# Attention and two expert layers on one core: another order of the opening's loads, more buffers for the first block, weights of the first pair in halves, a decode without its clamp

## The chip, the cores and the metric

The kernel runs on one core of one Trainium2 chip. The metric is the device time of one execution in microseconds (us). A core has TensorE (PE, matrix products; its weight loads are shown as PEld), VectorE (DVE), ScalarE (ACT), GpSimd (POOL) and SyncE (SP), which here only issues transfers. Each engine works through its own list of instructions in the order in which they were written, and waits on semaphores. Transfers run on 16 DMA engines.

## The reference

Three parts follow each other. Attention over 4 batches, 8 heads, 576 positions and 64 columns for a head adds a coarse part (means over 4 positions, full attention over 144 of them, each result used 4 times) and a local part (positions less than 4 apart):

```python
out_d = sm_attn(q_d, k_d, v_d)          # q_d ...: means over 4 positions
out_up = np.repeat(out_d, factor, axis=2)
mask = np.abs(pos[:, None] - pos[None, :]) < factor
...
return (out_up + out_local).astype(np.float32)
```

Its output is 2304 tokens of 512 columns. The first layer computes `g = h * tanh(softplus(h))` with `h = x @ w_in` (512 to 2048 columns) and `g @ w_out`. The second computes `h * softmax(h)` with 1024 columns, a layer norm with gain and a last product. The weights arrive as 64-bit floats, the rest as 32-bit.

## The kernel before, in words

The 2304 tokens are 18 units of 128 tokens; `BLOCKS = [4, 3, 3, 4, 4]` gathers them into five blocks. For each block the attention (`local`, per unit; `coarse`, per batch and pair of heads p) writes x into a tile as a high and a low part. Then 16 slots follow, one for each 128 columns of the 2048 (f = 0 to 15): `chunk_in` multiplies (L630, 12 matmuls: 4 pieces of the contraction, 3 products of high and low parts) and runs the activation on ACT and DVE, and `chunk_out` multiplies back (L658, 12 matmuls). `SEGS` runs block 0 with f = 0 to 9 first (slots 0 to 9), then all of block 1 (slots 10 to 25), then the rest of block 0 and the other blocks. The second layer (`tile_in`, `tile_out`) comes last.

**Weights.** Two values of f share a tile, a pair j. `first_weights` loads the 64-bit words of a pair (1 MB for `wi`, 1 MB for `wo`), `decode` makes 32-bit floats of them with an activation and four DVE passes (L540 is the clamp, L544 a shift, L546 and L548 bring in other bits), and `split` (L552, L553) makes the high and the low part. Pairs 0 to 4 are needed in slots 0 to 9, pairs 5, 6 and 7 from slots 20, 22 and 24. A load waits for the decode two tiles before it (`pace`).

**One local unit.** Loads of k, q (L321, L322) and four small ones of v (L326); 64 small matmuls for the scores (L352); mask, maximum, exponentials (L373) and norm on DVE and ACT; four transposes (L391); 64 small matmuls for the values (L409); the sum with the coarse part (L419); high part (L430) and low part (L432) of x. The first block's units ("early") share two score tiles and write their values to two PSUM banks with the tag "at". The values of a unit need all four coarse parts of its batch.

**One coarse part of batch 0.** Loads of q and k (L450) and, for two p at once, of v (L452); sums over 4 positions on DVE (L453 to L460); scores (L483, 12 matmuls), maximum, exponentials (L490), norm (L498), six transposes (L512), values (L525, 8 matmuls), copy (L529). For block 1 and later the sums over 4 positions are done by transfers that accumulate, issued by POOL (L263).

**The order of the work.** `Plan` keeps every operation with its engine, an estimated cost, a due time in slots ("want") and its buffers. `Plan.run` plays the program once with these costs: each engine always takes the ready operation with the lowest due time whose buffers are free. The resulting order is what is written, engine by engine. So the constants `CLOAD0`, `LOAD0`, `COARSE0`, `LOCAL0` and their spacings (opening), `NEXT` (attention of the next block) and `WANT` (weight pairs) set the order and nothing else; due times of the opening are negative. Transfers of SP go to one queue in order of issue.

## Time and profile before

| | us |
|---|---|
| median of 3 runs | 742.5 (737.35 to 745.17) |
| profiled execution, whole | 748.06 |
| its span, first to last instruction | 745.9 |
| PE busy | 700.8 |
| DVE busy | 475.3 |
| ACT busy | 485.7 |

The span is that of the profiled execution and is what views of the trace are measured in. Busy time of PE is modelled for pipelined matmuls and is no measure of how full the array is. "<-issue" behind an idle time says that the engine waited for nothing that the profile shows.

### The profile page before, as it was taken

How to read it: one execution, taken by the hardware profiler on the slowest of the kernel's cores; microseconds unless marked ns; L12 is line 12 of the kernel's file. 1: busy time of each engine (PE TensorE's matmuls, PEld its weight loads, DVE VectorE, ACT ScalarE, POOL GpSimd, SP SyncE). 2: the span in 40 equal slices, each digit the busy share in tenths (PEclk: the TensorE clock that was granted, in tenths of full speed). 3: DMA queues.
4: the chain of work that ended last, by engine and by line, in shares of the span. 5: the costliest groups of instructions: out<-in, count | busy, mean ns of one | idle time of the engine just before them, and what ended most of it. 6: DMA issues, size and time to landing. Idle time of an engine off the chain costs nothing.

```text
span 745.9 us, 14393 instructions
## 1 busy us (share of the span) xinstructions
PE 700.8 (94%) x5584; PEld 589.1 (79%) x5584; DVE 475.3 (64%) x1038; ACT 485.7 (65%) x1143; POOL 71.6 (10%) x86
## 2 busy tenths in 40 slices
PE   3656998999989999999999999999999999999997
PEld 2445676889988899999788888888888788888886
DVE  6767997597745536765656655655556776666662
ACT  2764977677767667786766856776754555555542
POOL 2031343012420002120000000000000000000000
PEclk9656999999989999999999999999999999999999
DMA  8887676466633127761524223310415534443331
GB/s 245 260 232 209 145 169 159 157 155 152 126 61 107 55 46 178 182 156 58 177 80 134 69 93 125 121 50 11 145 59 168 161 130 162 141 155 129 128 139 43
DMA packets 75532, 98.35 MB, mean 132 GB/s; under 512 B 6536, under 2 KB 58120, under 8 KB 75464
## 3 DMA queue, kind: packets, MB, share of 16 engines
q1 hardware_dynamic: 63432, 83.61, 35.4%
q0 software_dynamic: 9440, 9.10, 8.7%
q10 hardware_dynamic: 2592, 4.72, 1.6%
q8 instruction: 44, 0.72, 0.4%
q14 instruction: 24, 0.20, 0.1%
HBM read 73.81 MB, written 23.59 MB: 131 GB/s over the span
## 4 chain that ended last, share of the span: by engine, by line
PE 85%; DVE 4%; ACT 4%; DMA 4%; issue 2%; SPq 1%; ACTq 0%
PE h L630 26%; PE y L658 25%; PE at L808 12%; PE y L699 12%; PE at L409 3%; DMA ku<-in_ku_dram 2%; PE at L699 1%; DMA g<-in_qu_dram 1%; PE at L352 1%; PE at L483 1%; SPq L265 1%; PE at L525 1%; PE at L512 1%; DMA vu<-in_vu_dram 1%; PE at L391 1%
## 5 line engine op out<-in xcount | busy, mean ns | idle before, releaser
L630 PE MATMUL h<-x,wi 128*128 128x512 f32 (+1 forms) x960 | 217.7, 377 | 6.5 <-DVE e L644 6.5
L658 PE MATMUL y<-g,wo 128*128 128x512 f32 (+1 forms) x960 | 218.2, 375 | 0.0
L630 PEld LDWEIGHTS h<-x,wi 128*128 128x128 f32 x960 | 176.3, 191 | 33.3 <-DVE e L644 8.6
L658 PEld LDWEIGHTS y<-g,wo 128*128 128x128 f32 x960 | 174.5, 190 | 24.4 <-issue 1.6
L808 PE MATMUL at<-wi,wo 128*128 128x512 f32 x432 | 100.6, 389 | 0.0
L808 PEld LDWEIGHTS at<-wi,wo 128*128 128x128 f32 x432 | 81.0, 188 | 16.8
L699 PE MATMUL y<-wi,raw 128*128 128x512 f32 x384 | 89.9, 390 | 1.1 <-DVE raw L691 1.1
L638 ACT ACTIVATE e<-h 128x512 f32<-128x512 f32 (+1 forms) x80 | 44.2, 552 | 66.0 <-PE h L630 65.4
L699 PEld LDWEIGHTS y<-wi,raw 128*128 128x128 f32 x384 | 71.9, 188 | 16.7 <-DVE raw L691 1.5
L644 DVE SCALAR_TENSOR_TENSOR e<-e,h 128x512 f32<-128x512 f32 (+1 forms) x80 | 50.3, 630 | 32.0 <-ACT e L643 31.3
L647 DVE TENSOR_TENSOR g<-e,g 128x512 fp32r<-128x512 f32 (+1 forms) x80 | 50.6, 634 | 23.9 <-ACT g L646 23.4
L639 DVE TENSOR_SCALAR e<-e 128x512 f32<-128x512 f32 (+1 forms) x80 | 31.8, 398 | 53.3 <-ACT e L638 53.2
L640 ACT ACTIVATE e<-e,ones 128x512 f32<-128x512 f32 (+1 forms) x80 | 54.3, 680 | 17.3 <-DVE e L639 16.9
L646 ACT CAST g<-e 128x512 fp32r<-128x512 f32 (+1 forms) x80 | 45.9, 575 | 28.2 <-DVE e L644 27.9
L642 ACT ACTIVATE e<-e,ones 128x512 f32<-128x512 f32 (+1 forms) x80 | 54.2, 679 | 1.7
L263 POOL DMA_DIRECT2D qkd<-in_qkc_dram x36 | 35.6, 992 | 141.1 <-DMA qkd<-in_qkc_dram 84.3
L643 ACT ACTIVATE e<-e 128x512 f32<-128x512 f32 (+1 forms) x80 | 46.9, 586 | 1.1
L263 POOL DMA_DIRECT2D vd<-in_vc_dram x36 | 36.3, 1028 | 58.0 <-DMA vd<-in_vc_dram 48.0
L373 ACT ACTIVATE sm<-sm,nm 128x40 f32<-128x40 f32 x120 | 37.6, 315 | 4.6 <-DVE nm L367 4.6
L813 ACT COPY ys<-at 128x512 f32<-128x512 f32 x18 | 10.6, 589 | 41.3 <-PE at L808 41.3
L725 ACT ACTIVATE wo<-y,nm 128x1024 f32<-128x1024 f32 x16 | 17.9, 1118 | 22.3 <-DVE nm L723 22.3
L540 DVE TENSOR_SCALAR ys<-ys 128x512 f32<-128x512 f32 (+1 forms) x36 | 18.6, 517 | 17.4 <-ACT ys L539 17.3
(155 smaller groups left out, 822.2 us busy)
## 6 DMA issues: line engine op xcount, KB each, us to landing
raw<-in_w_dram SPq DMA_DIRECT2D x24, 512.0 KB
zscr<-wo SPq DMA_DIRECT2D x17, 512.0 KB
wo<-zscr SPq DMA_DIRECT2D x68, 128.0 KB
wi<-in_w_dram SPq DMA_DIRECT2D x6, 1024.0 KB
wo<-in_w_dram SPq DMA_DIRECT2D x6, 1024.0 KB
qkd<-in_qkc_dram POOLq DMA_DIRECT2D x36, 144.0 KB, 4.3
ku<-in_ku_dram SPq DMA_DIRECT2D x15, 320.0 KB
vu<-in_vu_dram SPq DMA_DIRECT2D x60, 80.0 KB
```

What stands on the lines that cost most here:

```text
L263: return op("pool", nbytes / DMA_RATE, want, lambda: nc.gpsimd.dma_start(out_(), in_(), accum_op=ALU.add), r, w, after=after)
L630: mm(h()[:, :N], w()[:, f % 2, a, 128 * c:128 * c + 128], x()[:, b, c, :N], start=(n == 0), stop=(n == 11))
L638: act(act_us(N), s + 0.1, lambda: nc.scalar.activation(e(), h()[:, :N], AF.Exp), [h], [eb])
L640: act(act_us(N, 0.09), s + 0.1, lambda: nc.scalar.activation(e(), e(), AF.Square, bias=ones()[:, 0:1]), [ones], [eb])
L642: lambda: nc.scalar.activation(e(), e(), AF.Ln, scale=0.5, bias=ones()[:, 1:2]), [ones], [eb])
L643: act(act_us(N), s + 0.1, lambda: nc.scalar.activation(e(), e(), AF.Exp, scale=-1.0), [], [eb])
L644: dve(dve_us(N), s + 0.2, lambda: nc.vector.scalar_tensor_tensor(e(), e(), 1.0, h()[:, :N], op0=ALU.subtract, op1=ALU.mult), [h], [eb])
L646: act(act_us(N), s + 0.2, lambda: nc.scalar.copy(g()[:, 0, :N], e()), [eb], [g])
L647: dve(dve_us(N), s + 0.2, lambda: nc.vector.tensor_tensor(g()[:, 1, :N], e(), g()[:, 0, :N].bitcast(F32), op=ALU.subtract), [eb], [g])
L658: mm(y[d2]()[:, d, :N], w()[:, f % 2, a, c:c + 128], g()[:, b, :N], start=(f == fs[0] and n == 0), stop=(f == fs[-1] and n == 2))
L699: mm(part(m), x()[:, a, c, :], w()[:, i, b, :], start=(n == 0), stop=(n == 11))
L808: mm(o(), ln()[:, a, k, :], w()[:, i, b, :], start=(n == 0), stop=(n == 23))
```

## The change

The seven coarse loads of batch 0 are issued as one group ahead of the units' loads, with due times of their own; the weights of pair 0 come after the units, each in two halves with decode and split of their own, so that a slot needs only the half that it reads. The four early units have a score tile each (one of its own and three parts of one tile), pairs of small columns each, and the odd ones write their values into a "y" PSUM tile instead of two "at" banks. The norm of the early coarse parts goes from DVE (L498) to ACT, as three activations with a scale for each partition. `decode` drops the clamp: the activation multiplies by 2^-112 instead of taking the absolute value, and the two bit masks are adapted. All constants of the order are new. In `Plan`, small transfers of POOL (the masks) no longer take the place of others in the played program, and a tile is held as long as one of its parts is.

The diff, cut to its core:

```diff
-LEAD = 2.5
-EARLY = -84
-CLOAD0 = -90
-LOAD0 = -86
-EI = 2.5
-COARSE0 = -80
-CSPC = 5.0
-CDT = 2
-LOCAL0 = -76
-LSPC = 4.0
-CLOAD = 4.0
+LEAD = 2.2
+EARLY = -95.5
+CLOAD0 = -108.6
+VLOAD = [-115.1, -87.3]
+LOAD0 = -77.4
+FIRST = {'wi': (-67.7, -66.3), 'wo': (-64.9, -40.0)}
+EI = 9.9
+COARSE0 = -111.0
+CSPC = 1.1
+CDT = 7.9
+LOCAL0 = -105.5
+LSPC = 1.4
+CLOAD = 12.8
...
-NEXT = {0: (0.0, 6.0, -3.0, 0.8), 26: (-3.0, 4.0, -14.0, 2.0), 32: (2.0, 10.0, 4.0, 1.2), 48: (2.0, 10.0, 4.0, 1.2)}
-WANT = [0, 2, 4, 6, 8, 13, 16, 20]
+NEXT = {0: (0.6, 7.5, -8.4, 0.2), 26: (-4.7, 4.4, -13.4, 0.2), 32: (-3.9, 7.5, -5.0, 1.7), 48: (1.4, 10.4, 2.8, 3.4)}
+WANT = [6.9, 4.6, 4.5, 5.8, -4.5, 13.8, 34.8, 28.7]
...
+SHIFT = 2.0 ** -112
...
+        bufs.update({id(b.of): b.of for b in list(bufs.values()) if isinstance(b, View)})
...
+                        if eng == "pool" and cost < 0.1:
+                            heapq.heappush(done, (at[eng] + 3.0, pick, False))
+                            continue
...
-    sms = [S([UQ, 2, 2, 2, 64], *t) for t in (("sm0", 1), ("wi", 8))]
+    sms = [S([UQ, 2, 2, 2, 64], "sm0", 1)]
+    smw = S([UQ, 3, 2, 2, 2, 64], "wi", 8)
+    sms += [View(smw, lambda t, i=i: t[:, i]) for i in range(3)]
+    small = S([UQ, 96], "nm", 2)
...
-        tl = LOAD0 + LSPC * u if early else t0 - 2.5
+        tl = LOAD0 + 3.0 * u if early else t0 - 2.5
...
-        sm = sms[u % 2 if soon else 0]
+        sm = sms[u if early else u % 2 if soon else 0]
...
-        nm = S([UQ, 96], "nm", 2)
-        su = S([UQ, 16], "su", 2)
+        if early:
+            nm, su = (View(small, lambda t, c=c: t[:, c:c + 8]) for c in (16 * u, 16 * u + 8))
+        else:
+            nm = S([UQ, 96], "nm", 2)
+            su = S([UQ, 16], "su", 2)
...
-        o = [P("at"), P("at")]
+        if early and u % 2:
+            oy = P("y")
+            o = [View(oy, lambda t, par=par: t[:, par]) for par in range(2)]
+            of = [oy]
+        else:
+            o = of = [P("at"), P("at")]
...
-            dma(CLOAD0 + p, qk4, lambda: qkc[0, :, :, p].rearrange("r d s t -> d r s t"), w=[qk4], nbytes=589824)
-            if p % 2 == 0:
-                dma(CLOAD0 + p + 0.5, v8, lambda: vc[0, :, :, p:p + 2].rearrange("r k p g d -> k r p g d"), w=[v8], nbytes=589824)
...
-        dve(dve_us(432), t0 + 0.4 * dt, norm_b, [su], [smb])
+        def norm_c():
+            for c in range(3):
+                nc.scalar.activation(sm()[:, c, :], sm()[:, c, :], AF.Copy, scale=su()[:, c:c + 1])
+
+        if early:
+            act(0.7, t0 + 0.4 * dt, norm_c, [su], [smb])
+        else:
+            dve(dve_us(432), t0 + 0.4 * dt, norm_b, [su], [smb])
...
-        act(act_us(n), want, lambda: nc.scalar.activation(xf(), high().bitcast(F32), AF.Abs), [raw], [x])
+        act(act_us(n), want, lambda: nc.scalar.activation(xf(), high().bitcast(F32), AF.Copy, scale=SHIFT), [raw, *hold], [x])
         dve(dve_us(n, True), want, lambda: nc.vector.tensor_scalar(
-            xf(), xf(), HIGH_MIN, HIGH_MAX, op0=ALU.max, op1=ALU.min), [], [x])
-
-
-        dve(dve_us(n, True), want, lambda: nc.vector.tensor_scalar(
-            xi(), xi(), 3, 0x3FFFFFF8, op0=ALU.logical_shift_left, op1=ALU.bitwise_and), [], [x])
+            xi(), xi(), 3, 0x7FFFFFF8, op0=ALU.logical_shift_left, op1=ALU.bitwise_and), [*hold], [x])
...
+    def opening_weights(tag, src, want):
+
+        w = S([128, 2, 2, 512], tag, 8, F32R)
+        x = S([128, 2, 512], "ys", 2)
+        raw = S([128, 2, 512, 2], tag, 8, I32)
+        for i in range(2):
+            ri, xi, wv = (View(b, lambda t, i=i: t[:, i]) for b in (raw, x, w))
+            dma(FIRST[tag][i], ri, lambda i=i: words(src[:, i], "k (n two) -> k n two"),
+                r=[raw, w], w=[ri], nbytes=524288)
+            last = decode(xi, lambda t: t, ri, 512, want + i, [x, raw])
+            act(act_us(512), want + i + 0.1, lambda xi=xi, wv=wv: nc.scalar.copy(wv()[:, 0], xi()), [xi, x, w], [wv])
+            dve(dve_us(512), want + i + 0.1, lambda xi=xi, wv=wv: nc.vector.tensor_tensor(
+                wv()[:, 1], xi(), wv()[:, 0].bitcast(F32), op=ALU.subtract), [xi, x, w], [wv])
+            ready_w[tag, i] = [wv]
+        pace.append(last)
+        return w
...
+        qk4s.append(S([128, 4, 2, 144], *(("x1", 1), ("x0", 1), ("wo", 8), ("wo", 8))[p]))
+        dma(CLOAD0 + 0.1 * p, qk4s[p], lambda p=p: qkc[0, :, :, p].rearrange("r d s t -> d r s t"), w=[qk4s[p]], nbytes=589824)
+    for i in range(2):
+        v8s.append(S([72, 4, 2, 2, 128], "wo", 8))
+        dma(VLOAD[i], v8s[i], lambda i=i: vc[0, :, :, 2 * i:2 * i + 2].rearrange("r k p g d -> k r p g d"), w=[v8s[i]], nbytes=589824)
```

## Rows read from the trace of the kernel before

**Rows 1.** Page: busy time of the engines; shares of the chain that ended last.
```profile
PE 700.8 (94%) x5584; PEld 589.1 (79%) x5584; DVE 475.3 (64%) x1038; ACT 485.7 (65%) x1143; POOL 71.6 (10%) x86
...
PE 85%; DVE 4%; ACT 4%; DMA 4%; issue 2%; SPq 1%; ACTq 0%
```

**Rows 2.** Busy time by stretches: stretch, length, engines, TensorE clock, DMA share, GB/s.
```profile
0.00:30.00 30.00, 15.92 (x231) 10.86 (x232) 20.53 (x47) 11.02 (x38) 4.57 (x12) 0.93 0.94 265
30.00:65.30 35.30, 18.03 (x533) 14.53 (x530) 25.60 (x53) 22.71 (x95) 10.82 (x12) 0.50 0.85 226
65.30:139.30 74.00, 69.70 (x589) 54.56 (x588) 56.30 (x101) 55.89 (x134) 21.73 (x24) 0.94 0.60 146
139.30:225.40 86.10, 82.66 (x557) 77.40 (x557) 62.67 (x125) 64.24 (x152) 21.45 (x24) 0.96 0.57 138
225.40:745.90 520.50, 514.53 (x3683) 431.75 (x3681) 310.25 (x716) 331.84 (x727) 13.03 (x14) 1.00 0.37 115
```

**Rows 3.** TensorE's timeline, opening: start, us, operation, count, idle before it and releaser.
```profile
27.19 0.93 PE L352 MATMUL y<-g 64*32 64x40 f32 x64 [0.86 <-DMA g<-in_qu_dram]
...
37.72 0.85 PE L409 MATMUL at<-wo,vu 40*64 40x32 f32 x19 [0.28 <-issue]
39.92 1.11 PE L391 MATMUL h<-ident,wi 128*128 128x128 f32 x4 [1.34 <-DVE wi L383]
40.96 0.94 PE L352 MATMUL y<-wi 64*32 64x40 f32 x64
41.83 1.28 PE L409 MATMUL at<-wo,g 40*64 40x32 f32 x39
46.62 0.87 PE L409 MATMUL at<-wo,g 40*64 40x32 f32 x25 [3.51 <-issue]
...
64.62 0.71 PE L352 MATMUL at<-ku,qu 64*32 64x40 f32 x36 [3.32 <-issue]
65.26 7.98 PE L630 MATMUL h<-x,wi 128*128 128x512 f32 x24
```

**Rows 4.** DMA view, instruction queue: whole span; then 34:36, 43:45, 62:65, 65:67.
```profile
q8 instruction: 44, 0.72, 0.4%
...
q8 instruction: 1, 0.02, 3.2%
...
q8 instruction: 1, 0.02, 2.9%
...
q8 instruction: 1, 0.02, 2.0%
...
q8 instruction: 1, 0.02, 3.0%
```

**Rows 5.** SP's timeline: issue of the fourth unit's values.
```profile
33.12 3.46 SPq L265 DMA_DIRECT2D wi<-in_vu_dram  x4
```

**Rows 6.** DVE's timeline: the first pass over loaded data.
```profile
5.39 0.76 DVE L453 TENSOR_TENSOR x<-x 128x576 f32<-128x576 f32 x1 [3.41 <-DMA x<-in_qkc_dram]
```

**Rows 7.** Groups by line and shape: busy us, mean ns of one; idle before, releaser.
```profile
L540 DVE TENSOR_SCALAR ys<-ys 128x1024 f32<-128x1024 f32 x12 | 8.4, 700 | 3.7 <-ACT ys L539 3.7
L546 DVE SCALAR_TENSOR_TENSOR ys<-wi,ys 128x1024 int32<-128x1024 int32 x6 | 7.4, 1235 | 0.1
L553 DVE TENSOR_TENSOR wi<-ys,wi 128x1024 fp32r<-128x1024 f32 x16 | 19.5, 1221 | 9.3 <-ACT wi L552 9.3
L498 DVE TENSOR_TENSOR wo<-wo,csu 128x432 f32<-128x432 f32 x8 | 4.8, 603 | 0.1
L490 ACT ACTIVATE wo<-y,cnm 128x144 f32<-128x144 f32 x12 | 4.4, 377 | 11.8 <-DVE cnm L503 11.8
```

**Rows 8.** TensorE's timeline later on: two waits for DVE.
```profile
76.67 3.02 PE L630 MATMUL h<-x,wi 128*128 128x512 f32 x12 [1.81 <-DVE e L644]
...
208.51 2.98 PE L630 MATMUL h<-x,wi 128*128 128x384 f32 x12 [1.95 <-DVE e L644]
```

More of the change, by code (lines that the diff above doesn't have):

```diff
@@ L1 @@
 import heapq
-import struct
 from contextlib import ExitStack
@@ L410, in values @@
                                at()[r, 2 * h2 + a, GQ * g:GQ * g + GQ], start=True, stop=True)
-        passed["x", u] = pe(1.2 if early else 0.7, t0 + 0.7 * dt, values, [v, at] + ups, o + [xf], after=gate_x)
+        passed["x", u] = pe(1.9 if early else 0.7, t0 + 0.7 * dt, values, [v, at] + ups, of + [xf], after=gate_x)
         for par in range(2):
@@ L423, in add @@
                         op=ALU.add)
-            dve(dve_us(256) + 0.04, t0 + 0.8 * dt, add, [o[par]] + ups, [xf])
+            dve(dve_us(256) + 0.04, t0 + 0.8 * dt, add, [of[par % len(of)]] + ups, [xf])
         x = xt[i]
@@ L434 @@
     v8s = []
+    qk4s = []
     def coarse(b, p, t0, dt):
@@ L442, in coarse @@
         if early:
-            qk4 = S([128, 4, 2, 144], *(("x1", 1), ("x0", 1), ("wo", 8), ("wo", 8))[p])
-            if p % 2 == 0:
-                v8s.append(S([72, 4, 2, 2, 128], "wo", 8))
+            qk4 = qk4s[p]
             v8 = v8s[p // 2]
@@ L529, in coarse, with decode @@
         act(0.17, t0 + 0.8 * dt, lambda: nc.scalar.copy(up[b]()[:, p, :], o()[:, :144]), [o], [up[b]])
-    def decode(x, part, raw, n, want):
+    def decode(x, part, raw, n, want, hold=()):
         low = lambda: raw()[..., 0]
@@ L537, in decode @@
         xi = lambda: part(x()).bitcast(I32)
[L539 removed]
+        act(act_us(n), want, lambda: nc.scalar.activation(xf(), high().bitcast(F32), AF.Copy, scale=SHIFT), [raw, *hold], [x])
         dve(dve_us(n, True), want, lambda: nc.vector.tensor_scalar(
[L541 to L545 removed]
+            xi(), xi(), 3, 0x7FFFFFF8, op0=ALU.logical_shift_left, op1=ALU.bitwise_and), [*hold], [x])
         dve(dve_us(n), want, lambda: nc.vector.scalar_tensor_tensor(
[L547 removed]
+            xi(), low(), 29, xi(), op0=ALU.logical_shift_right, op1=ALU.bitwise_or), [raw, *hold], [x])
         return dve(dve_us(n), want, lambda: nc.vector.scalar_tensor_tensor(
[L549 removed]
+            xi(), high(), -0x80000000, xi(), op0=ALU.bitwise_and, op1=ALU.bitwise_or), [raw, *hold], [x])
     def split(w, x, want):
@@ L560 @@
     pace = []
+    ready_w = {}
+    def opening_weights(tag, src, want):
[13 more added lines that the diff above has]
+        return w
     def first_weights(j, tag, src, want, after):
@@ L632, in g1 @@
                     n += 1
-        g1_op[s] = pe(12 * (N + 32) / 2400, s, g1, [w, x], [h], after=[g1_op.get(s - 1)])
+        g1_op[s] = pe(12 * (N + 32) / 2400, s, g1, [w, x, *ready_w.get(("wi", f), [])], [h], after=[g1_op.get(s - 1)])
         eb = S([128, NMAX], "e", 3)
@@ L659, in g2 @@
                            start=(f == fs[0] and n == 0), stop=(f == fs[-1] and n == 2))
-            pe(6 * (N + 32) / 2400, s + 1.7, g2, [w, g], [y[d2]])
+            pe(6 * (N + 32) / 2400, s + 1.7, g2, [w, g, *ready_w.get(("wo", f), [])], [y[d2]])
     def block_end(i, s, N, y, more):
@@ L829 @@
     for p in range(4):
+        qk4s.append(S([128, 4, 2, 144], *(("x1", 1), ("x0", 1), ("wo", 8), ("wo", 8))[p]))
[3 more added lines that the diff above has]
+        dma(VLOAD[i], v8s[i], lambda i=i: vc[0, :, :, 2 * i:2 * i + 2].rearrange("r k p g d -> k r p g d"), w=[v8s[i]], nbytes=589824)
+    for p in range(4):
         coarse(0, p, COARSE0 + CSPC * p, CDT)
@@ L836, in pair @@
         s = WANT[j] - LEAD
-        wi[j] = first_weights(j, "wi", w1[2 * j:2 * j + 2].rearrange("f k c x -> k f (c x)"), s, late)
-        wo[j] = first_weights(j, "wo", w2[256 * j:256 * j + 256, :].rearrange("(f k) n -> k f n", f=2), s + 1.5, late)
+        first = first_weights if j else lambda j, tag, src, s, late: opening_weights(tag, src, s)
+        wi[j] = first(j, "wi", w1[2 * j:2 * j + 2].rearrange("f k c x -> k f (c x)"), s, late)
+        wo[j] = first(j, "wo", w2[256 * j:256 * j + 256, :].rearrange("(f k) n -> k f n", f=2), s + 1.5, late)
     for j in range(8 - WORES):
```

7 lines of the change are left out of this document (removed).

## The prediction, made before the result was known

> **What bounds the kernel now.** I read the page first. TensorE is busy for 94% of the span and carries 85% of the chain that ended last [rows 1]. The busy time by stretches then parts the span in two [rows 2]: from the first matmul of the expert layer (L630, at 65.26 us [rows 3]) TensorE is busy 69.70 of 74.0, 82.66 of 86.1 and 514.53 of 520.5 us, 666.9 of 680.6 us together. Ahead of it lie 65.3 us with only some 34 busy. So the time is "when the first L630 starts" plus about 680 us that TensorE itself fills, and an opening that ends x us sooner is worth x us, unless the weights or the second block's attention then come late.
>
> What ends last in the opening? Not the data alone. DMA engines are busy for 0.94 of the first 30 us and 0.85 of the next 35 [rows 2]. The surprise is in TensorE's timeline [rows 3]: it stops for 3.51 us in the middle of the 64 equal matmuls of L409, and for 3.32 us in the middle of the 64 of L352, with the releaser "issue", which means that nothing in the program was waited for. Count the matmuls: from 37.72, where a short stop of 0.28 us ends, to 46.62 there are 19+4+64+39 = 126. From 46.62 to 64.62 there are 253 (the row at 46.62 with its 25, five rows with 200, then 28 of L352 in two rows), twice 126. Each goes with a weight load, so one stop falls every 252 TensorE instructions (a few semaphore instructions beside them). The instruction queue of the DMA view moves 0.72 MB in 44 packets [rows 4], 16 KB each, and 5584 matmuls with 5584 loads make 254 instructions for each packet. One packet lies ahead of each stop's end: in 34 to 36, 43 to 45 and 62 to 65 us [rows 4]. So TensorE fetches its program in blocks of 126 matmuls, the next block is fetched only when one is entered, and while the data queues are full that small packet waits. Call the entries B2 (matmul 219, near the end of the row at 27.19, at about 28.0: 124 matmuls in five rows lie between that row and the one at 37.72), B3 = 37.72, B4 = 46.62, B5 halfway, B6 = 64.62. One block takes (64.62 - 28.0)/4 = 9.2 us, and every one of these entries came when the packet came or just behind it. After 64.62 the next packet comes by 67 [rows 4]: the wait belongs to the full queues. The opening of before runs at the pace of this fetch, from 28 us to its end.
>
> **The change, part by part.**
>
> *Loads.* The seven coarse loads (3.5 MB) and the four units (3.67 MB) now go ahead of both weights of pair 0 (1.05 MB each). At the 265 GB/s of the first 30 us [rows 2] the fourth unit's data have landed by 7.27/0.265 = 27.4 us; before, its values were only issued from 33.12 us on [rows 5], so it has its data some 10 us sooner. Unit 1 no longer stands behind 1.05 MB of weights, 4.0 us.
>
> *Buffers.* Four score tiles, four pairs of small columns and PSUM of its own for the odd units' values take away the serial order of units (two score tiles, two "at" banks before). Their cost is two more memsets, in DVE's idle time before 5.39 us, where it waits for the first data 3.41 us [rows 6]: nothing, and less than 1 us if that cover were gone.
>
> *Weights in halves.* The same work in pieces of 512 columns. Of pair 0 the first half alone is needed for slot 0, so 524 KB more of loads, 2 us, after the units: 29.4 us, hidden behind the units' own work.
>
> *Coarse norm to ScalarE.* L498 leaves DVE (0.603 us, four times), three activations like L490's (0.377 us each) come on ACT [rows 7]: 1.1 us on ACT against 0.6 us on DVE. In the opening ACT is busy 11.02 of the first 30 us [rows 2], and the coarse work is done before the fetch sets the pace: nothing; 0.5 us for each of four if it did not hide, 2.1 us.
>
> *Decode without its clamp.* One of the two fast passes goes: 0.700 us for 12 tiles of 1024 columns and, half as long, for 24 of 512, some 18 us of DVE. The multiply takes the place of Abs in an activation of the same shape: nothing. Ten of the 12 fall into the first ten slots. But DVE is busy 56.30 of 74.0 us there, TensorE 69.70 [rows 2]: TensorE hides nearly all. What can show are the waits for DVE, 1.81 us at 76.67 [rows 8]. Bounds 0 and 1.8 there; I take 1.0, as a decode pass stands between the passes that this wait ends with.
>
> *Order (WANT, NEXT, VLOAD ...).* The coarse work of block 1 gets an earlier due time, its units are spread wider, pairs 6 and 7 a much later one. Two waits of TensorE of this kind stand in the trace, 1.81 and 1.95 us [rows 8]: both gone is -3.8, the same again is +3.8. I take 0.
>
> *The sum.* The 632 matmuls that slot 0 needs (104 coarse, four units of 64+4+64) are the same as before, so B2 to B5 must all be entered first. B2: before 28.0; at best 4.0 earlier, with unit 1; I take 26.0, halfway, since the block ahead of it has to be fetched too. Three blocks at 9.2 give B5 = 26.0+27.5 = 53.5. I keep the 9.2: the queue is as full as before, with the weights of pairs 0 and 1 and block 1's loads now behind the units. After B5 come 35 matmuls of unit 3's values (39 take 1.28 us, so 1.15 [rows 3]), three elementwise passes of at most 0.7 us (estimated from the 0.700 of a larger tile [rows 7]), and about 1 us for the order: 4 us. First L630 at 57.5 us. Before it stood at 65.26, after all 64+64 score matmuls of two units of block 1, hence behind B6. I expect one of them ahead of it now (632+64 = 696, under 723). Gain 65.26 - 57.5 = 7.8, and 1.0 of the decode: 8.8 us. B6 then falls at about 62.7, while slot 0 and 1 keep TensorE busy until 65 (24 matmuls take 7.98 us [rows 3]), and hides.
>
> The profiled execution took 748.06 us (745.9 us of span and 2.16 around), 5.6 above the median of the runs. 748.06 - 8.8 = 739.3 on its footing; on the median's, 742.5 - 8.8 = 733.7. A per cent, 7.4 us, is about what a measurement of this kernel tells from no change.
>
> **Rivals.**
>
> *The fetch hides.* If the data queue is short when a block is entered, the packet comes within 2.4 us, as the one after 64.62 [rows 3, 4], and no entry waits. The engines' work then sets the start: DVE was busy 20.53 of the 24.6 us from its first data to 30 us (0.83), and 46.1 us until 65.3; without pair 1's decodes and split (two of 0.7+0.7+1.2+1.2 and 1.2, about 9) and some 3 us of what the change drops or moves, 34 us. 5.4+34/0.83 = 46.4 us: 18.9 sooner, with the decode 742.5 - 19.9 = 722.6. For it: the small loads of the units leave fewer bytes in flight. Against it: all four periods of before, and the loads are now packed tighter. The Trainium skill (Runtime: NRT & Kernel Launch, Instruction fetch mechanics) would have it this way: it calls crossing a 16 KB boundary "mostly hidden". The trace agrees with the block size and not with the hiding: 3.51 and 3.32 us in the open.
>
> *The opening is rebuilt, but B6 still stands ahead of slot 0.* If the earlier due time of coarse 1 or two units' scores puts over 91 more matmuls before the first L630, it starts at 26.0+4x9.2 = 62.8 plus some 0.7: gain 1.8, with the decode 2.8: 739.7. For it: that is what before does. Against it: unit 5's loads wait for unit 4's scores, and slot 0 is ready sooner.
>
> *Slower.* Pairs 6 and 7 are due at 32.6 and 26.5 in the planner's time but used in slots 22 to 25. Where a decode is late, g1 stands for the rest of it: 1.2+0.7+1.2+1.2, and the cast, 5 us. In 139 to 225 us, where this happens, DVE and ACT are busy 62.67 and 64.24 of 86.1 [rows 2], and a wait of 1.95 us stands there already, so there is room. All four tiles late: 20 us, 754. It makes the kernel slower once the lateness passes the 8.8 gained.
>
> **Chances and range.** Forecast 0.48 (its own range 728 to 739: 1.3 us either way for each block, 3.8 for the order), B6 ahead 0.24 (736 to 744), fetch hidden 0.16 (718 to 728), slower 0.12 (745 to 757). Range 722 to 747: it leaves out about half of the fetch-hidden case and most of the slower one. Faster by over 1% (under 735.1): two thirds of the forecast, 0.33, and 0.16, with 0.01 of the second rival: 0.50. Within 1%: 0.15+0.22: 0.37. Slower: 0.11 of the last and 0.02 of outliers: 0.13.
>
> **What would show it.** In TensorE's timeline of the changed kernel: stops with "issue" every 126 matmuls in 28 to 60 us, and an instruction packet 2 to 3 us ahead of each one's end; if there are none and L630 starts before 50, the first rival holds. The start of L630, against 57.5, is the largest term. The fourth unit's scores should come by about 30 us; if they come at 40, the loads are not where I put them. TensorE's busy time from its first L630 to the end should stay near 667 us; waits on ACT or DVE over 2 us around slots 20 to 25 are the last rival. The clamp's group must be gone and DVE's busy time down by about 20 us.

## The result and the profile after

| us | before | after |
|---|---|---|
| median of 4 runs each | 740.85 (737.35 to 745.17) | 731.17 (728.09 to 732.64) |
| profiled execution, whole | 748.06 | 731.20 |
| its span | 745.9 | 729.4 |
| DVE busy | 475.3 | 458.0 |
| ACT busy | 485.7 | 489.9 |

The ratio of after to before is 0.987, with an interval of 0.983 to 0.992: 9.7 us of the median (before's 740.85 is of four runs; the 742.5 that the prediction went by was of three of them). The prediction said 733.7, 8.8 us less, with a range of 722 to 747. The time lies near the forecast. Its terms do not, as the rest shows: against two executions of before's order in which TensorE had no stops the opening gained far less than the sum says, and the two terms taken as 1 and 0 (decode and order) came out larger.

The page of after, busy time of the engines and the chain that ended last, beside [rows 1]:

```profile
PE 692.7 (95%) x5584; PEld 583.3 (80%) x5584; DVE 458.0 (63%) x1008; ACT 489.9 (67%) x1159; POOL 71.3 (10%) x86
...
PE 84%; DMA 6%; DVE 3%; SPq 2%; ACT 2%; issue 1%; POOL 0%; POOLq 0%; ACTq 0%
```

Busy time by stretches of after, columns as in [rows 2]. The bounds are the first matmul of slot 0 (54.40), of slot 10, where block 1 begins (129.20), and of slot 26 (209.40); in the profiled execution of before these three stood at 65.3, 140.2 and 225.4.

```profile
0.00:30.00 30.00, 15.52 (x294) 11.07 (x295) 18.71 (x51) 17.59 (x82) 4.59 (x12) 0.94 0.85 239
30.00:54.40 24.40, 13.24 (x471) 11.08 (x469) 19.64 (x44) 18.10 (x66) 8.68 (x10) 0.64 0.91 254
54.40:129.20 74.80, 70.95 (x617) 55.40 (x613) 61.01 (x105) 60.42 (x139) 24.01 (x27) 0.98 0.71 180
129.20:209.40 80.20, 80.20 (x674) 75.39 (x673) 58.46 (x121) 66.39 (x168) 21.11 (x24) 1.00 0.62 155
209.40:729.40 520.00, 512.78 (x3542) 430.39 (x3540) 300.17 (x690) 327.39 (x706) 12.90 (x14) 0.99 0.37 114
```

So 10.9 us of the 16.5 between the two spans are there at slot 0, 11.0 at slot 10 and 16.0 at slot 26. The fourth line is the surprise: TensorE does not wait at all in slots 10 to 25. In before it waited 3.4 us there, twice for the pass of DVE that ends the activation; [rows 8] has one of the two. It is also at full clock there (1.00 against 0.96), and it does more small matmuls of later attention (674 matmuls against 557 [rows 2]).

TensorE's timeline of after in the opening (columns as in [rows 3]; L358 are scores, L420 values, L659 the first matmuls of the expert layer):

```profile
27.61 0.86 PE L358 MATMUL y<-wi 64*32 64x40 f32 x64 [1.39 <-DMA wi<-in_qu_dram]
...
31.69 0.77 PE L358 MATMUL y<-wi 64*32 64x40 f32 x64 [0.57 <-DMA wi<-in_qu_dram]
...
32.97 1.29 PE L420 MATMUL at<-wo,vu 40*64 40x32 f32 x64
...
37.45 1.06 PE L420 MATMUL y<-wo,g 40*64 40x32 f32 x28 [0.72 <-issue]
41.31 2.03 PE L420 MATMUL at<-wo,wi 40*64 40x32 f32 x64 [2.80 <-ACT wo L401]
...
45.50 0.54 PE L358 MATMUL at<-ku,qu 64*32 64x40 f32 x33 [0.28 <-issue]
45.97 1.93 PE L420 MATMUL y<-wo,wi 40*64 40x32 f32 x64
53.52 0.93 PE L358 MATMUL at<-ku,qu 64*32 64x40 f32 x64 [5.62 <-DVE su L385]
54.38 1.65 PE L659 MATMUL h<-x,wi 128*128 128x512 f32 x3
...
64.33 3.03 PE L659 MATMUL h<-x,wi 128*128 128x512 f32 x12 [1.95 <-DVE e L673]
```

Four units follow each other faster: the fourth one's scores stand at 31.69. Program blocks of 126 matmuls begin at 27.65, 32.08, 37.45, 45.50 and 53.75, so the periods are 4.4, 5.4, 8.0 and 8.3 us, where the prediction put 9.2 for each. Only 1.0 us of stops with "issue" is left of the 7.1 in [rows 3]. In their place stands one wait of 5.62 us, ahead of the 64 scores of unit 5 (block 1), and those scores stand ahead of slot 0 in TensorE's order. The last values of unit 3 end at 47.90; slot 0 starts 6.5 us later.

DVE's timeline in that wait: three passes of the weights (L554 shift, L585 low part, L556 other bits) stand ahead of the low part of x (L443) that slot 0 waits for.

```profile
49.03 0.68 DVE L554 TENSOR_SCALAR ys<-ys 128x1024 int32<-128x1024 int32 x1
49.63 0.68 DVE L585 TENSOR_TENSOR wo<-ys,wo 128x512 fp32r<-128x512 f32 x1
50.23 1.22 DVE L556 SCALAR_TENSOR_TENSOR ys<-wi,ys 128x1024 int32<-128x1024 int32 x1
51.37 0.68 DVE L443 TENSOR_TENSOR x<-e,x 128x512 fp32r<-128x512 f32 x1
```

x is ready at 51.37 + 0.68 = 52.05, and slot 0 starts 2.3 us after that, behind unit 5's scores. SP's timeline shows those scores' own data:

```profile
22.67 3.21 SPq L268 DMA_DIRECT2D wi<-in_vu_dram  x4
...
26.97 3.21 SPq L268 DMA_DIRECT2D wi<-in_vu_dram  x4
30.23 0.96 SPq L268 DMA_DIRECT2D wi<-in_w_dram  x2
...
46.14 0.38 SPq L268 DMA_DIRECT2D ku<-in_ku_dram  x1
46.57 0.49 SPq L268 DMA_DIRECT2D qu<-in_qu_dram  x1
```

The load of unit 5's q is issued at 46.57, after unit 4's scores gave its tile back, and its last semaphore update in the trace comes at 53.39, 0.13 us ahead of the scores. The releaser printed, DVE's L385, ends at 53.43 and belongs to unit 4. The trace settles whose wait it is: TensorE's own wait instruction ahead of these scores names the semaphores of the loads of k and q, and it starts at 53.41, behind the load's last update and ahead of the end of L385. The first rows show another limit: each load of v (80 KB) keeps SP's queue busy for 0.8 us, four in 3.21 us, so the loads of the third and of the fourth unit take about 4.3 us each to issue, while the DMA engines are busy for 0.79 of 20 to 30 us.

### The profile page after: what moved, and what is told of

Its sections match the earlier page's. It is cut to its first block, busy times and chain, and to the rows that moved or that the text cites. A ratio compares the mean times of both kernels' runs of the same rounds, so it can differ in the third digit from the quotient of the medians.

```text
span 729.4 us, 14381 instructions
## 1 busy us (share of the span) xinstructions
PE 692.7 (95%) x5584; PEld 583.3 (80%) x5584; DVE 458.0 (63%) x1008; ACT 489.9 (67%) x1159; POOL 71.3 (10%) x86
## 4 chain that ended last, share of the span: by engine, by line
PE 84%; DMA 6%; DVE 3%; SPq 2%; ACT 2%; issue 1%; POOL 0%; POOLq 0%; ACTq 0%
PE y L687 26%; PE h L659 25%; PE at L837 13%; PE y L728 12%; DMA qkd<-in_qkc_dram 3%; SPq L268 2%; PE at L420 2%; PE at L728 1%; DMA qu<-in_qu_dram 1%; PE at L490 1%; PE at L358 1%; DMA vd<-in_vc_dram 1%; PE at L397 1%; PE at L539 1%; PE at L526 1%
## 5 line engine op out<-in xcount | busy, mean ns | idle before, releaser
L659 PE MATMUL h<-x,wi 128*128 128x512 f32 (+1 forms) x960 | 213.4, 373 | 2.1 <-DVE e L673 2.1
L659 PEld LDWEIGHTS h<-x,wi 128*128 128x128 f32 x960 | 174.2, 189 | 26.8 <-DVE e L673 3.3
L671 ACT ACTIVATE e<-e,ones 128x512 f32<-128x512 f32 (+1 forms) x80 | 54.4, 680 | 1.7
L379 ACT ACTIVATE sm<-sm,nm 128x40 f32<-128x40 f32 x112 | 35.1, 316 | 0.7 <-DVE nm L373 0.6
L554 DVE TENSOR_SCALAR ys<-ys 128x512 int32<-128x512 int32 (+1 forms) x38 | 18.8, 495 | 19.7 <-ACT ys L553 19.3
```

Source lines behind the costliest of these rows:

```text
L659: mm(h()[:, :N], w()[:, f % 2, a, 128 * c:128 * c + 128], x()[:, b, c, :N], start=(n == 0), stop=(n == 11))
L671: lambda: nc.scalar.activation(e(), e(), AF.Ln, scale=0.5, bias=ones()[:, 1:2]), [ones], [eb])
```

## The experiments

The table has every kernel that was profiled, ordered by span. "x of unit 6" is when DVE starts the last part of x that slot 10 reads, a pass of 0.7 us. The ratio is of medians, the other columns are of the one profiled execution: b_order's took 3.7 us less than its median, b_again's 3.3 us more.

| kernel | ratio to before (95%) | span | slot 0 | x of unit 6 | slot 10 | slot 10 to end | TensorE busy |
|---|---|---|---|---|---|---|---|
| after | 0.987 (0.983 to 0.992) | 729.4 | 54.4 | 128.2 | 129.2 | 600.2 | 692.7 |
| a_order | 0.995 (0.990 to 0.999) | 731.6 | 51.1 | 131.8 | 132.6 | 599.0 | 698.4 |
| b_noclamp_fix | 0.995 (0.991 to 0.999) | 733.0 | 57.1 | 130.1 | 130.7 | 602.3 | 697.3 |
| b_shift2 | one run | 733.2 | 58.0 | 128.5 | 129.1 | 604.1 | 703.0 |
| a_clamp_fix | 0.996 (0.992 to 0.999) | 733.2 | 54.2 | 131.5 | 132.5 | 600.7 | 695.6 |
| b_order | 1.009 (1.004 to 1.014) | 738.7 | 56.6 | 142.4 | 143.1 | 595.6 | 700.9 |
| a_u5late | 1.002 (0.999 to 1.006) | 740.4 | 51.8 | 142.9 | 144.2 | 596.2 | 700.6 |
| b_again (before) | 1.002 (0.997 to 1.006) | 742.9 | 64.3 | 135.2 | 135.8 | 607.1 | 699.5 |
| a_clamp | 1.009 (1.004 to 1.013) | 743.6 | 49.2 | 140.2 | 142.9 | 600.7 | 704.8 |
| a_wfirst | 1.007 (1.003 to 1.012) | 744.0 | 56.4 | 142.1 | 145.9 | 598.1 | 703.1 |
| before | 1 | 745.9 | 65.3 | 139.6 | 140.2 | 605.7 | 700.8 |
| b_shift | one run | 746.7 | 69.8 | 140.9 | 141.4 | 605.3 | 711.1 |
| a_two | 1.017 (1.010 to 1.025) | 747.6 | 52.6 | 154.4 | 155.9 | 591.7 | 702.8 |
| b_noclamp | 1.015 (1.008 to 1.022) | 747.9 | 60.9 | 147.0 | 148.4 | 599.5 | 703.0 |

**Are the stops bound to places in the program?** b_shift puts extra small matmuls, whose result nothing reads, ahead of all of TensorE's work in before, so that every block boundary moves to another matmul:

```diff
+    def extra():
+        for _ in range(63):
+            mm(warm()[:64, :32], ..., start=True, stop=True)
+
+    pe(3.0, -98, extra, [sms[0]], [warm])
```

> The kernel before, with 63 small matmuls (32 columns, on a tile of zeros, their result unused) put ahead of everything on TensorE; the order of the opening is otherwise the same. Theory 1 (the stops in the opening are TensorE waiting for the next block of its program): a block is 126 matmuls, so 63 more move each stop half a block ahead in the program. The stop of 3.5 us that was behind 39 of the 64 value matmuls of unit 1 (L409) is gone from there and stands inside the 64 score matmuls of unit 3 (L352), and the one of 3.3 us inside unit 5's scores is gone and stands inside unit 3's values; an instruction packet lies 2 to 3 us ahead of each one's end. Theory 2 (the stops belong to data or a semaphore at that place, and the count of 126 is chance): they stay at the 39th value matmul of unit 1 and the 28th score matmul of unit 5. Either way the first L630 starts at 62 to 67 us.

Measured: 748.82, slot 0 at 69.8. But each call of a small matmul appears twice in the trace: the 63 calls are 126 matmuls, a whole block, and the boundaries fell two matmuls from where they were before. The run can't tell a place in the program from a place in time. With 126 more matmuls slot 0 stood 4.5 us later, and the longest stop, 3.07 us, stood at the boundary where before has 0.28 us; the one of 3.51 us had shrunk to 1.23 us. b_shift2 has 31 calls, 62 matmuls, half a block:

> The kernel before with 31 small matmuls ahead of everything on TensorE, which the trace counts as 62 (the 63 of the run before were 126 in the trace, a whole block, so that stops could not move); the order of the opening is otherwise the same. Theory 1 (a stop every 126 matmuls is TensorE waiting for its program): the stops move half a block back in the program. None is left behind the 39th value matmul of unit 1 nor the 28th score matmul of unit 5; stops of over 1 us with no releaser lie at about the 41st score matmul of unit 3, the 35th of unit 4 or the 29th value matmul of unit 3. Theory 2 (they belong to data or a semaphore): they stay. First L630 at 62 to 68 us either way.

Measured: 735.35, 4.1 below the median of before's runs beside it (739.46), with 62 matmuls more; as one run it lies inside their range (734.56 to 749.12). Slot 0 at 58.0 is outside what either theory expected. TensorE's timeline of b_shift2 has no stop with "issue" from 20 to 60 us, neither at the old boundaries nor at the moved ones:

```profile
42.21 1.93 PE L409 MATMUL at<-wo,g 40*64 40x32 f32 x64
...
57.16 0.93 PE L352 MATMUL at<-ku,qu 64*32 64x40 f32 x62 [0.59 <-DVE e L419]
58.02 7.43 PE L630 MATMUL h<-x,wi 128*128 128x512 f32 x24
```

Are the stops then an accident of the one execution that was profiled? The kernel before, unedited, profiled again:

> The kernel before once more, with no edit: what does a second profile of it show? Theory A (the two stops at TensorE's program blocks, 3.5 us at 42.8 and 3.3 us at 61.0, belong to the execution that was profiled; most executions of before have little or none of them): the first g1 stands at 56 to 60 us, slot 10 at 129 to 133, and the profiled time is 733 to 741 us, near the 735 of the half-block shift. Theory B (the stops are part of every execution of this program, and the old decoding without its clamp, or the shift, took them away): the first g1 stands at 64 to 66 us, slot 10 at 139 to 141, and the profiled time is 744 to 750 us. Both expect a ratio of 1.000 with 1 inside the interval; the spread of its runs, 735 to 750, is the spread that any small edit is measured against.

Measured: 741.66 (734.90 to 744.99 over ten runs); the profiled execution took 744.99, and its opening is that of theory B:

```profile
37.65 0.85 PE L409 MATMUL at<-wo,vu 40*64 40x32 f32 x19 [0.39 <-issue]
...
46.82 0.87 PE L409 MATMUL at<-wo,g 40*64 40x32 f32 x25 [3.79 <-issue]
...
63.68 0.71 PE L352 MATMUL at<-ku,qu 64*32 64x40 f32 x36 [1.95 <-issue]
64.32 2.07 PE L630 MATMUL h<-x,wi 128*128 128x512 f32 x4
```

The same two matmuls stop again (39 and 25 of one group, 28 and 36 of the other), for 3.79 and 1.95 us. So the place belongs to the program and the length to the execution. b_noclamp_fix (below), whose matmuls stand in before's order without a shift (its decode is the new one), has no stop with "issue" from 18 to 75 us either: the shift was not needed to be rid of them. Theory A named a slot 0 of 56 to 60 and fell there. Theory B does not hold whole either, as slot 10 came at 135.8. Whether the executions of this program that take 735 us have the stops is not shown, since its two profiled executions took 748 and 745. What speaks for shorter stops there: the mean granted clock is lower in before's longer runs, 0.979 in one of 731.90 us and 0.968 in one of 742.84, and the 0.50 of the clock lies mainly in the opening [rows 2].

**Which part of the new opening brings it?** Three edits undo one part of after each. Every edit changes what the planner plays, so it writes another order, for the whole first half. a_wfirst issues the weights of pair 0 among the units' loads:

```diff
-FIRST = {'wi': (-67.7, -66.3), 'wo': (-64.9, -40.0)}
+FIRST = {'wi': (-76.0, -75.9), 'wo': (-73.0, -72.9)}
```

> The changed kernel with only the due times of pair 0's loads moved back to where they stood before: wi's halves between units 0 and 1, wo's between units 1 and 2. Theory 1 (what the new order of loads does is to keep the data queue short while the units come, because their small loads are issued slowly, and so the instruction packets come sooner): with 2 MB of weights among the units the packets wait 4 to 8 us again instead of 1 to 6, stops with no releaser of 2 us and more come back, and the first matmul of the expert layer starts 4 to 9 us later than the 54.4 of the changed kernel; the time is 735 to 741. Theory 2 (the buffers are what matters, the order of loads is only the units' data some us later): no such stops beyond 1 us, start at 54 to 57, time 731 to 734.

Measured: 745.67, above both theories. Slot 0 is 2.0 us later than in after, as the second has it; four stops with "issue" (0.34, 1.38, 0.47 and 1.79 us) stand where after has 1.0 us, more than the second allows and less than the first. But slot 10 is 16.7 later. a_two gives the early units two score tiles again:

```diff
-        sm = sms[u if early else u % 2 if soon else 0]
+        sm = sms[u % 2 if soon else 0]
```

> The changed kernel with two score tiles for the four early units instead of four (units 2 and 3 use those of 0 and 1 again); all else as in the changed kernel, so far as the planner's order allows. Theory 1 (loads and the fetch): units 2 and 3 wait for the transposes of 0 and 1, which come at 31 and 33 us, while their data come at 27.6 and 31.7; the loss is 1 to 4 us in the start of the expert layer, time 731 to 736. Theory 2 (buffers): the units run in pairs one behind the other, as before; the start falls back by 8 us or more, time 738 to 743.

Measured: 750.76, with slot 0 at 52.6, earlier than in after, and slot 10 at 155.9. So the four tiles are not needed for an early slot 0, in the order that the planner then writes, and both theories miss the time. One matmul block was entered late in it; most of the loss is in the later part:

```profile
52.14 0.54 PE L358 MATMUL at<-ku,qu 64*32 64x40 f32 x33 [2.85 <-issue]
...
154.16 1.78 PE L539 MATMUL at<-atT,vd 72*64 72x144 f32 x8
155.88 2.61 PE L659 MATMUL h<-x,wi 128*128 128x384 f32 x7
```

Up to 156 us TensorE still works at attention of later units that after does behind slot 10, and slot 0 to slot 10 takes 103.3 us with 15.4 of them idle. a_u5late tests my first reading of after, that unit 5's scores cost 2.3 us where they stand. They, and those of unit 6, must come behind the first matmuls of slot 0; the loop that plans block 1 moves behind the planning of slot 0, and one argument is added:

```diff
-                local(u0 + j, t0, 5, gate)
+                    local(u0 + j, t0, 5, gate, [g1_op[0]] if nxt == 1 and j > 0 else [])
```

> The changed kernel with one dependency more: the scores of block 1's second and third units wait in the planner for the first matmuls of slot 0 (the attention of block 1 is planned one slot later in the program text, with the same due times). In the changed kernel the last part of x is ready at 52.05 us, yet TensorE starts the expert layer at 54.38, behind 64 score matmuls that begin at 53.52. Theory A (those scores wait for the load of q, issued at 46.57, and hold up the expert layer): the start moves to 52 to 53 us; time 728 to 731 if the scores then cost their 0.9 us later on. Theory B (the start is set by something else, as DVE's passes on the weights, which the profile names as the releaser): it stays at 54 or later and the time within 1 us of 731.

Measured: 741.47, no faster than before. TensorE's timeline of a_u5late:

```profile
51.76 0.80 PE L659 MATMUL h<-x,wi 128*128 128x512 f32 x1 [2.84 <-ACT x L441]
...
80.69 0.78 PE L358 MATMUL at<-ku,qu 64*32 64x40 f32 x64
...
135.55 1.09 PE L397 MATMUL at<-ident,sm 128*128 128x128 f32 x4 [2.08 <-ACT e L672]
...
144.24 1.92 PE L659 MATMUL h<-x,wi 128*128 128x384 f32 x10
```

Slot 0 does start 2.6 us sooner, as soon as x allows. But unit 5's scores now come at 80.69 instead of 53.52, block 1's chain ends later, and slot 10 starts at 144.2, 15.0 us later. The first reading falls: theory A had the start about right and the time wrong, so a sooner slot 0 alone does not shorten the kernel. In all 14 profiles slot 10 follows the start of x of unit 6 by 0.5 to 3.8 us, and from there the rest takes 592 to 607 us. By slot 0 the order of the kernels would be another: a_clamp has the earliest (49.2) and a span of 743.6. Slot 10 is a mark that goes with the time, not by itself its cause: b_order has it at 143.1 and its span is 7.2 us shorter than before's, where it stands at 140.2.

**The same matmuls, at another clock.** All kernels but b_shift and b_shift2 run 5584 matmuls, yet TensorE is busy with them for 692.7 us in after and for 695.6 to 704.8 us in the others. Of the 16.5 us between the spans of before and after, 8.1 are busy time and 8.4 idle time. The openings of before and of after up to slot 0, and slots 0 to 9 of a_u5late (columns as in [rows 2]):

```profile
0.00:65.30 65.30, 33.95 (x761) 25.39 (x761) 46.13 (x99) 33.73 (x132) 15.39 (x24) 0.70 0.89 244
0.00:54.40 54.40, 28.76 (x761) 22.15 (x761) 38.35 (x94) 35.69 (x146) 13.27 (x22) 0.81 0.88 246
...
51.80:144.20 92.40, 81.72 (x688) 62.54 (x689) 65.69 (x115) 65.53 (x156) 27.85 (x31) 0.90 0.62 156
```

As many matmuls are busy 5.2 us less in after's opening, half of the 10.9 us at slot 0, with a granted clock of 0.81 against 0.70. Two rows of the opening above give the price: 64 matmuls of the values took 1.29 us at 32.97, at full clock (2.4 GHz), and 2.03 us at 41.31, at half (1.2 GHz; the last view of this document has the clock). a_u5late, a_clamp, a_wfirst and a_two are busy 7.9, 12.1, 10.4 and 10.1 us longer than after, of the 11.0, 14.2, 14.6 and 18.2 us by which their spans exceed its. From slot 0 to slot 10 their granted clock is 0.88 to 0.90, against 0.98 in after, and TensorE idles 7.8 to 15.4 us there, against 3.9. So more than half of what each of these four loses is longer busy time of the same matmuls, with a lower clock in a stretch in which TensorE also waits longer. Busy time is modelled, each figure is of one execution, and no run changes the waits or the clock alone: which of the two led to the other is not shown.

**Decode and order, each alone.** b_noclamp is before with the new decode, a_clamp is after with the old one, both with the order that the planner then finds. In b_noclamp:

```diff
-        act(act_us(n), want, lambda: nc.scalar.activation(xf(), high().bitcast(F32), AF.Abs), [raw], [x])
-        dve(dve_us(n, True), want, lambda: nc.vector.tensor_scalar(
-            xf(), xf(), HIGH_MIN, HIGH_MAX, op0=ALU.max, op1=ALU.min), [], [x])
+        act(act_us(n), want, lambda: nc.scalar.activation(xf(), high().bitcast(F32), AF.Copy, scale=SHIFT), [raw], [x])
```

> The kernel before with the new decode alone (no clamp pass, a multiply in place of the absolute value); the planner's costs change with it, so the order of the work shifts a little everywhere. Theory 1 (DVE is no bound, TensorE hides the 18 us that leave it): 739 to 743, as before, DVE busy 456 to 460 instead of 475. Theory 2 (the decode is a large part of what the change brings): 731 to 736.

> The changed kernel with the old decode (with its clamp pass) put back; opening, buffers and constants stay. Theory 1 (decode hidden): the first matmul of the expert layer at 54 to 57 us, as two passes of 512 columns stand ahead of it on DVE; time 731 to 735. Theory 2 (decode a large part): 737 to 741. Theory 3 (what counts is when block 1's coarse part is done and slot 10 starts, and any shift of the planned order moves that): the time follows the start of slot 10, 129 us in the changed kernel, 140 before, whichever way the decode goes.

Measured: 748.43 and 744.60, outside what theories 1 and 2 expected of either. Taking 13 us of DVE's work out of before makes it 1.5% slower (DVE busy 462.5 against 475.3), and putting it back into after costs 2.2% against after (1.0085/0.9872). The two can't both be the price of a clamp: in both, slot 10 moved by 8 to 14 us, with block 1's coarse part and values, as a_clamp's theory 3 has it. Next the constants: b_order is before with the new `NEXT`, `WANT` and `CLOAD`, a_order is after with the old `NEXT` and `WANT`:

```diff
-NEXT = {0: (0.6, 7.5, -8.4, 0.2), 26: ...
-WANT = [6.9, 4.6, 4.5, 5.8, -4.5, 13.8, 34.8, 28.7]
+NEXT = {0: (0.0, 6.0, -3.0, 0.8), 26: ...
+WANT = [0, 2, 4, 6, 8, 13, 16, 20]
```

> The kernel before with the changed constants for the later attention and the weight pairs (NEXT, WANT, CLOAD), its opening and decode as before. Theory 1 (the opening makes the gain): first L630 at 62 to 66 us, time 738 to 744. Theory 3 (an earlier due time for block 1's coarse part brings slot 10 forward): slot 10 starts at 130 to 136 us instead of 140, time 731 to 737.

> The changed kernel with the constants of before for the later attention and the weight pairs (NEXT, WANT), its opening and decode as changed. The planned order of the opening is the same up to the first matmul of the expert layer, which now stands ahead of unit 5's scores. Theory 1 (the opening makes the gain): first matmul at 52 to 55 us, time 730 to 735. Theory 3 (slot 10 waits for block 1's coarse part and its three units one behind the other): unit 5's scores come after 70 us, slot 10 starts at 140 or later, time 738 to 745, though the expert layer starts 10 us sooner than before.

Measured: 744.26 and 733.63. In b_order slot 0 came at 56.6 and slot 10 at 143.1, against both theories; a_order's time is that of theory 1, and its slot 10 at 132.6 is not that of theory 3. The new constants make the old opening 0.9% slower; in the new one after is 0.7% below a_order (0.9872/0.9945 = 0.993), which is not clear of noise, as the two intervals overlap. Their worth depends on the rest of the kernel and is not a number of its own.

**The decode in a fixed order.** So the order was held: in b_noclamp_fix the planner still plans the clamp, at its old cost and place, but nothing is written for it; in a_clamp_fix the clamp is written inside the operation of the shift, so that after's order stays.

```diff
-            xf(), xf(), HIGH_MIN, HIGH_MAX, op0=ALU.max, op1=ALU.min), [], [x])
+        dve(dve_us(n, True), want, lambda: None, [], [x])
```

> The kernel before in exactly its own order of work, with the new decode: the clamp's place in the plan stays with its cost, but issues nothing. Theory 1 (the clamp is hidden by TensorE): 738 to 742; first L630 within 1 us of 65, slot 10 within 2 us of 140. Theory 2 (the decode is worth 5 us and more by itself, and the 748 of the run before came of the other order): 732 to 736. Theory 3 (the other order alone made the 748): as theory 1.

> The changed kernel in exactly its own order of work, with the old decode: the clamp is issued together with the shift behind it, without a place of its own in the plan. Theory 1 (hidden): 731 to 735, first matmul of the expert layer at 54.5 to 57, slot 10 at 129 to 133. Theory 2 (decode worth 5 us and more): 736 to 742. Theory 3 (the 744.6 of the run with the clamp in the plan came of the other order): as theory 1, at least 8 us below it.

Measured: 737.12 and 735.83. With the order held, the decode is worth 0.5% in before's order (0.995, just under 1 at the interval's upper end) and 0.9% in after's (0.9872/0.9958; the two intervals meet at 0.992). Both times lie between the ranges of theories 1 and 2. b_noclamp_fix has slot 0 at 57.1 and slot 10 at 130.7, where theory 1 had 65 and 140; its opening has no stops. a_clamp_fix is 8.8 us below a_clamp, as theory 3 has it: the rest of a_clamp's loss came of its order. Of a_clamp_fix the stretches of slots 0 to 9 and 10 to 25, and TensorE's waits in the first of them (sum, count, longest):

```profile
54.20:132.50 78.30, 73.55 (x619) 57.00 (x613) 66.95 (x115) 61.74 (x140) 25.22 (x27) 0.95 0.68 174
132.50:215.00 82.50, 81.24 (x674) 75.36 (x673) 63.03 (x131) 66.04 (x168) 21.70 (x24) 1.00 0.60 150
...
PE h L672 <- DVE e L686: 1.9, 1, 1.9
...
PE y L700 <- DVE wo L576: 1.0, 1, 1.0
```

Against after (54.4, 74.8, 80.2): the same start, 3.5 us more in the first ten slots and 2.3 more in the next sixteen, while the rest is 1.8 us shorter (518.2 against 520.0). In the first stretch DVE is busy 5.9 us longer (66.95 against 61.01) and TensorE waits 1.0 us for the pass that makes the low part of the weights (L576), for which after does not wait; its idle time there grows from 3.85 to 4.75 us, and its own busy time by 2.6, part of it at a lower granted clock (0.95 against 0.98).

The same view of b_shift2 (slots 0 to 9, slots 10 to 25) and its waits in the second stretch give before's order without the stops:

```profile
58.00:129.10 71.10, 68.51 (x609) 53.34 (x601) 60.81 (x109) 56.83 (x136) 25.85 (x27) 0.98 0.69 166
129.10:212.80 83.70, 80.28 (x547) 75.47 (x545) 61.77 (x124) 63.34 (x150) 21.60 (x24) 0.98 0.57 141
...
PE h L630 <- DVE e L644: 3.4, 2, 1.9
```

Against it, after starts slot 0 3.6 us sooner, takes 3.7 longer for the first ten slots, 3.5 less for the next sixteen and 0.4 less for the rest (520.4 there): 3.8 us in all. Against b_noclamp_fix, the other profile of before's order without stops, after starts slot 0 2.7 us sooner and slot 10 1.5 sooner. So where the opening has no stops, half or all of its gain is used up before slot 10, and most of what stays is the 3.4 us of waits in slots 10 to 25. b_noclamp_fix still waits 2.8 us for the same pass there, and a_clamp_fix, with the old decode in after's order, waits 1.2 us, so these waits go mainly with the order. b_shift2 and a_clamp_fix both have the old decode and the same span, 733.2: against an execution without stops (which carries 62 more matmuls here), opening, buffers and order together show no gain without the new decode. Of the medians a_clamp_fix is 0.4% below before.

## Why the prediction was right, and where its steps were not

**The sum.** 7.8 for the opening and 1.0 for the decode made 8.8; measured 9.7 between the medians and 16.9 between the two profiled executions. The prediction put the sum on the median's footing and was near. But the profiled execution of before carries stops that differ between executions, and the sum treated it as the same thing 5.6 us later. The nearness is in part luck: against the executions of before's order without stops the opening is worth 1.5 us at slot 10, or nothing, where the sum has 7.8, while the decode, in it with 1.0, is worth 3.8 between two spans, and 3.4 us of waits went from slots 10 to 25, in it with 0, part of them with the decode.

**Pace of the fetch.** "I keep the 9.2: the queue is as full as before" failed. The periods were 4.4 to 8.3, the stops 1.0 us together. The entry of B2 was sized wrongly the other way: 27.65 instead of 26.0, since the block ahead was held by unit 2's data (1.39 us at 27.61), not by the fetch. The step counted bytes at 265 GB/s and put the fourth unit's data at 27.4 us; its last v load is only out of SP's queue at 30.18, as SP takes 0.8 us to issue each 80 KB, and its scores start at 31.69. The prediction counted what was ahead of a load in bytes, not in SP's own time. By the row of 0 to 30 us the engines moved 239 GB/s at a share of 0.85, against 265 at 0.94 [rows 2]. A shorter queue would explain packets that come sooner; no run changes the queue alone, so that is argued and not shown. Nor do full DMA engines by themselves make a stop, as "the wait belongs to the full queues" has it. From 42 to 58 us they are busier in b_noclamp_fix (first line, a share of 1.03 as the view gives it), which has no stop, than in b_again (0.93), which stops for 3.79 us there:

```profile
42.00:58.00 16.00, 11.08 (x329) 9.00 (x325) 12.89 (x28) 13.93 (x57) 7.15 (x8) 0.50 1.03 295
...
42.00:58.00 16.00, 7.63 (x206) 6.17 (x203) 9.29 (x23) 11.34 (x49) 8.42 (x10) 0.50 0.93 235
```

The Trainium skill (Runtime: NRT & Kernel Launch, Instruction fetch mechanics) calls the crossing of a 16 KB boundary mostly hidden. The runs show both: no stop in b_noclamp_fix and b_shift2 and 1.0 us of stops in after, but 0.3 to 3.8 us at a boundary in the two executions of before.

**What stands ahead of slot 0.** "I expect one of them ahead of it now" failed: unit 4's and unit 5's scores both stand there, 760 matmuls as in before, so the rival "B6 still stands ahead" had the order right. Its price, 62.8, rested on the same 9.2 and failed with it. B5 was entered at 45.5, 8.0 sooner than predicted, and the 4 us behind it became 8.9: 33 scores and 64 values (2.4 us) where 35 values (1.15 us) were counted, 2.3 us of DVE's weight passes ahead of x, and 2.3 us from x to slot 0 with the load and the scores of unit 5. Two errors of opposite sign gave 54.4 where 57.5 was written; that this is near is luck.

**"An opening that ends x us sooner is worth x us."** This is the step that failed most. Between the two profiled executions it held, with 10.9 us at slot 0 and 11.0 at slot 10. But against before's order without stops 3.6 us of a sooner slot 0 became nothing by slot 10, and 2.7 us became 1.5. a_u5late, a_two and a_clamp start slot 0 at 49 to 53 us and end 11 to 18 us later than after. The condition at the end of that sentence, that neither the weights nor the second block's attention come late, is where it fell, and I gave it no row: in these three slot 10 comes 15.0, 26.7 and 13.7 us later than in after, with the last part of block 1's x (coarse part, then values of units 4, 5 and 6 one behind another, then x) 0.5 to 3.8 us ahead of it, as in each profile. Nor are the 680 us behind slot 0 a constant. They are 675.0 in after, with TensorE busy for 663.9 where the prediction named 667, and the sum had no term for a clock that changes what the same matmuls take (7.9 to 12.1 us of busy time in these three).

**Decode, 1.0 with bounds 0 and 1.8.** Mis-sized in after's order: 3.8 us between the spans of a_clamp_fix and after, 4.7 between their medians. In before's order b_noclamp_fix and b_shift2 (62 matmuls more), neither with stops, have spans of 733.0 and 733.2: next to nothing. The bound was read from TensorE's waits alone: of the 3.8 us in after's order 0.9 are idle time, inside the bounds, and 2.9 are busy time of TensorE (695.6 against 692.7), for which the term had no place. DVE's busy time fell by 17.3 us, near the 18 worked out (a pass over 512 columns of before takes 0.426 us and not half of 0.700); 17.1 us lie between a_clamp_fix and after.

**Order, 0 with 3.8 either way.** Slots 10 to 25 lost all of their 3.4 us of waits. That is near the lower bound that the prediction named, but it is another pair of waits: the bound adds one of 1.81 us in the first ten slots [rows 8], and there after still waits 1.95 us (64.33).

**The last rival.** Late tiles of pairs 6 and 7 would show as waits around slots 20 to 25. There is none.

**What is left open.** Why b_shift2 and b_noclamp_fix had no stops in the executions that were profiled. Ten runs of b_noclamp_fix spread from 731.2 to 742.8, so it may well have them in others; then part of its 0.5% is not the decode's. For the 5.9 us by which the medians (9.7) exceed the 3.8 against b_shift2, shorter stops of after's program are the reading that fits: after's four runs spread over 4.6 us and a_order's ten over 5.7, the 16 shortest of before's 25 beside a_order over 10.9. It is not shown by a profile of an ordinary run of before. What the loads' order, the buffers, the halves of the weights and the norm on ACT are each worth is not shown either, since no run undid one of them in after's order.

## What to carry to other kernels

Compare when each profile passes a few fixed marks, here the first slots of the first and of the second block: what is won at one mark can be gone at the next. Beside the waits, compare how long TensorE is busy with the same matmuls, and its granted clock; here that was about half of the difference between the two profiles. Where a planner writes the order, hold the order when one part is tested: with a new order, dropping the same clamp seemed to lose 1.5% or to gain 2.2%, in a held one it gained 0.5 to 0.9%. And take the footing of a sum from more than one execution when a stop stands in it for which nothing in the program is named.

## What the runs showed of the hardware that I had not expected

- Stops of TensorE at its program's block boundaries stand at the same matmuls in two executions of one program, with other lengths (3.51 and 3.79; 3.32 and 1.95 us). They are absent in one execution with 62 matmuls more ahead of them (b_shift2) and in one with the same matmuls in the same order (b_noclamp_fix), with DMA engines no less full (0.91 of 30 to 58 us in b_shift2, 0.82 in before).
- One call of a small 32-bit matmul makes two matmuls and two weight loads in the trace: 31 calls raised the count from 5584 to 5646.
- SP's time to issue can count for more than the bytes: 0.80 us for each 80 KB of v, 4.3 us for a unit's 0.9 MB, with the DMA engines busy for 0.79 of 20 to 30 us in after.
- TensorE's clock fell from 2.4 to 1.2 GHz later in after than in before, where it is 0.50 from 30 us on [rows 2]. The last view, windows of after, shows it full while scores and values follow each other (busy 5.05 of 7.00 us) and at half in the stretch of stops and waits behind it (8.19 of 17.40):

```profile
30.00:37.00 7.00, 5.05 (x182) 4.03 (x181) 3.09 (x9) 4.92 (x21) 0.00 (x0) 0.99 0.90 304
37.00:54.40 17.40, 8.19 (x289) 7.05 (x288) 16.55 (x36) 13.18 (x45) 8.68 (x10) 0.50 0.91 233
```
